# Attention scores in one two-bank PSUM tile, v's product on four quadrants, and one written order for the first layer

## The chip, the cores and the metric

One Trainium2 chip, one core of it. The metric is the device time of one execution in microseconds (us). The engines are TensorE (PE for matmuls, PEld for its weight loads), VectorE (DVE), ScalarE (ACT), GpSimd (POOL) and SyncE (SP, which here only issues DMAs).

## What is computed

Three stages follow one another, all in fp32: chunked attention, a gated layer (`x @ w_a * x @ w_b @ w_out`), and a mixture of four experts. The first two are called the first layer here, the third the second layer. The reference, cut:

```python
# attention: 4 batches, 8 heads, 576 positions in chunks of 64, head size 64
scores = scale * np.matmul(q_c, k_c.transpose(0, 1, 2, 4, 3))
scores = scores - np.max(scores, axis=-1, keepdims=True)
attn = np.exp(scores)
attn = attn / (np.sum(attn, axis=-1, keepdims=True) + 1e-09)
x = np.matmul(attn, v_c)                       # -> 2304 tokens x 512
x = ((x @ w_a) * (x @ w_b)) @ w_out            # 512 -> 1536 -> 512
p = domain_probs / (domain_probs.sum(-1, keepdims=True) + 1e-09)
for e in range(4):                             # 512 -> 1024 -> 512
    out += p[:, e:e + 1] * (np.maximum(x @ w1[e], 0.0) @ w2[e])
```

## The kernel before

**Numbers.** Each fp32 operand of the large products is kept as two fp32r tiles, a high part (a ScalarE copy) and a low part (the rest, a VectorE or GpSimd subtraction). Each product is then three matmuls: high by high, high by low, low by high. Some products of larger blocks go by a Strassen scheme with seven products for eight (`seq`, L845; `a_steps`, L1030; `o_step`, L1145). The weights of the first layer come in as float64 words and are turned into fp32 on the chip (`from_f64`, L227: two ScalarE, three VectorE and one GpSimd instruction for each piece of 512 columns), then split (`split_w`, L257). The weights of the second layer are split, summed and stored to DRAM by small jobs (`prepare`, L355) beside the first layer, and are loaded back later.

**Attention.** The 2304 tokens are 18 tiles of 128. For one tile, `emit_S` (L534) writes the scores into two PSUM tiles of one bank each, one for each head of a pair: 16 matmuls of 64x64x64, each of which the trace shows as two instructions. `emit_A` (L548) takes, for each of the two PSUM tiles, a maximum along the row and a subtraction, so four VectorE instructions on 256 columns. `emit_exp` is ScalarE's. `emit_B` (L565) sums the rows, adds, takes the reciprocal on VectorE and multiplies on GpSimd. `emit_T` (L575) transposes on TensorE and copies back on ScalarE. `emit_V` (L614) multiplies by v into one PSUM bank; its output goes to the same half of the partitions as its input comes from, so of the four 64x64 quadrants of the array only the two on the diagonal are in use. Two splits of the result (high part on ScalarE at once, low part on VectorE later) give x.

**PSUM.** The eight banks are four tiles `pm` (scores, the gated layer's a and b) and four tiles `ps` (transposes, v's product, w_out's products, the warm-up).

**Order.** The order of the instructions is the order in which the Python calls are made; every engine runs its own in order. The start is written out by hand (from L1279), with 40 warm-up matmuls that compute nothing (`keep_warm`, L204) between the attention of tiles 0 to 4. After that, eleven spans of the first two of twelve blocks of the gated layer run; between the steps of a span whole attention tiles are put in (`attn_slot`, L645), and w_out's steps of the span before are spread among them. Then the other ten blocks run in pairs (F = 1 to 5, L1377). Preparing jobs for the second layer come at written due counts (`WHEN`, L387; `tick`, L422, counts the steps). The jobs of the second layer itself (`part_of_h`, L1007: high and low parts of its hidden values, and sums) come when a small planner (`Plan`, L46) that follows instructions with estimated durations finds their engine free and their inputs ready.

Of the kernel before, what the change touches and what calls it, by code (L numbers as in the profile page):

```python
# [8 lines left out]
F32 = mybir.dt.float32  # L9
# [8 lines left out]
P = 128  # L18
# [3 lines left out]


DMA_US = 6.0
# [4 lines left out]
class Queue:  # L29
    def __init__(self, plan, name, engine):  # L30
        self.plan, self.name, self.engine = plan, name, engine

    def __getattr__(self, op):
        call = getattr(self.engine, op)

        def go(*args, **kw):
            aps = [x for x in (*args, *kw.values()) if isinstance(x, bass.AP)]
            out = kw.get("out", aps[0])
            ins = [x for x in aps if x is not out]
            self.plan.note(self.name, op, out, ins)  # L40
            return call(*args, **kw)  # L41

        return go


class Plan:  # L46


    LEAD = dict(PE=0.05, DVE=0.03, ACT=0.03, POOL=0.08, SP=0.05)

    def __init__(self, nc):
        self.nc = nc
        self.at = dict(PE=0.0, DVE=0.0, ACT=0.0, POOL=0.0, SP=0.0, port=0.0)
        self.written, self.read, self.writer, self.rings = {}, {}, {}, {}
        self.vector = Queue(self, "DVE", nc.vector)
        self.scalar = Queue(self, "ACT", nc.scalar)
        self.gpsimd = Queue(self, "POOL", nc.gpsimd)
        self.tensor = Queue(self, "PE", nc.tensor)
        self.sync = Queue(self, "SP", nc.sync)

    def __getattr__(self, name):
        return getattr(self.nc, name)

    def ring(self, tag, tile, n):

        names = self.rings.setdefault(tag, [])
        if len(names) >= n:
            old = names[-n]
            self.read[tile.tensor.name] = max(self.read.get(old, 0), self.written.get(old, 0))
        names.append(tile.tensor.name)  # L70
        return tile

    def cost(self, name, op, out, ins):

        n = out.free_size()
        psum = [x.space == bass.MemoryType.PSUM for x in (out, *ins)]
        if name == "PE":
            return ins[-1].free_size() / 2400 + 0.0134, False
        if name == "ACT":
            return (0.157 + n * 0.00084 if any(psum) else 0.172 + n * 0.00088), False  # L80
        if name == "POOL":
            return 0.18 + n * 0.00218, True
        n = max([n, *(x.free_size() for x in ins)])
        if any(psum):
            return 0.158 + n * 0.00104, False
        two = sum(x.free_size() > 1 for x in ins) > 1
        return (0.158 + n * 0.00104 if two else 0.15 + n * 0.00052), True

    def start(self, name, op, out, ins):
        t = self.at[name]  # L90
        deps = [self.written.get(x.tensor.name, 0) for x in ins]
        if self.writer.get(out.tensor.name) != name:
            deps.append(self.written.get(out.tensor.name, 0))
        deps.append(self.read.get(out.tensor.name, 0))
        t = max(t, max(deps) + self.LEAD[name])
        if self.cost(name, op, out, ins)[1]:
            t = max(t, self.at["port"])
        return t

    def note(self, name, op, out, ins):  # L100
        t = self.start(name, op, out, ins)
        if op == "dma_start":
            self.at[name] = t + 0.36
            end = t + DMA_US
        else:
            us, port = self.cost(name, op, out, ins)
            end = t + us
            self.at[name] = end if name == "PE" else end - 0.06
            if port:
                self.at["port"] = end - 0.14  # L110
            if name == "PE":
                end += 0.17
        self.written[out.tensor.name] = max(end, self.written.get(out.tensor.name, 0))
        self.writer[out.tensor.name] = name
        for x in ins:
            self.read[x.tensor.name] = max(end, self.read.get(x.tensor.name, 0))
# [3 lines left out]
def fused_kernel(  # L120
# [11 lines left out]

    nc = plan = Plan(tc.nc)
# [22 lines left out]
    ps_p = first.enter_context(tc.tile_pool(name="ps", bufs=4, space=bass.MemoryType.PSUM))  # L169
    early = ctx.enter_context(ExitStack())  # L170
    at_p = early.enter_context(tc.tile_pool(name="at", bufs=2, side="right"))
    st_p = early.enter_context(tc.tile_pool(name="st", bufs=3, side="right"))
# [3 lines left out]
    def psum():  # L176
        return plan.ring("ps", ps_p.tile([P, 512], F32, tag="ps", name="ps"), 4)

    def psum_m():
        return plan.ring("pm", psm_p.tile([P, 512], F32, tag="pm", name="pm"), 4)  # L180
# [23 lines left out]
    def keep_warm(n):  # L204

        ps = psum()
# [20 lines left out]
    def from_f64(r):  # L227
# [4 lines left out]
        nc.scalar.activation(out=low.bitcast(I32), in_=low, func=ACTF.Copy, scale=2.0**-29)  # L232
        nc.vector.tensor_single_scalar(out=high, in_=high, scalar=0x80000000, op=ALU.bitwise_and)
# [10 lines left out]
        )  # L244
        nc.gpsimd.tensor_tensor(
            out=t.bitcast(I32), in0=t.bitcast(I32), in1=low.bitcast(I32), op=ALU.add
        )
        load_w()
        return t
# [23 lines left out]
    def raw2_tile(name):  # L273
        return plan.ring("raw2", raw_p.tile([P, 1024], F32, tag="raw2", name=name, bufs=1), 1)
# [10 lines left out]
    def hi2(n, k):  # L285
        if nxt["prep"] == len(pieces):
            t = plan.ring("raw", raw_p.tile([P, 2, 512], F32R, tag="raw", name="made"), 2)
        else:
            t = plan.ring("made", made_tile(), 3)
        made[n, k] = t  # L290
        split_hi(t[:, 0, :], half(n, k))
# [11 lines left out]
    def sums2(n, x):  # L303
# [9 lines left out]
        if SUMS == "DVE":  # L313
            add_sb(o, y, z, op)
        else:
            nc.gpsimd.tensor_tensor(out=o, in0=y, in1=z, op=op)

    SUMS = "POOL"
    jobs = []
    EARLY = dict(ACT=0.05, POOL=1.8, DVE=0.05)  # L320
    SLACK = dict(ACT=0.9, POOL=3, DVE=0.9)

    class Job:
        def __init__(self, q, go, after=(), ready=lambda: 0, when=lambda: True, rank=0):
            self.q, self.go, self.after = q, go, after
            self.ready, self.when, self.rank, self.done = ready, when, rank, False
            jobs.append(self)

        def run(self):
            if not self.done:  # L330
# [3 lines left out]
                jobs.remove(self)  # L334
                self.go()

        def fits(self, now):
            if not (self.when() and all(j.done for j in self.after)):
                return False
            free = max(plan.at[self.q], plan.at["port"] if self.q != "ACT" else 0)  # L340
            if free > now + SLACK[self.q]:
                return False
            return self.ready() <= max(free, now) + EARLY[self.q]

    def written(tile):
        return plan.written.get(tile.tensor.name, 0)

    def over(tile):
        return max(written(tile), plan.read.get(tile.tensor.name, 0))

    def old(tag, back):
        return max([0] + [plan.read.get(x, 0) for x in plan.rings.get(tag, [])[-back:][:1]])


    def prepare(n, first):  # L355

        def fresh():
            return old("raw", 2) if nxt["prep"] == len(pieces) else old("made", 3)

        def job(q, go, after, ready):  # L360
            return Job(q, go, after, ready, rank=1)

        raw = lambda: written(raw2[n])
        before = job("ACT", lambda: load_raw2(n), first, lambda: old("raw2", 1))
        his, los = {}, {}
        stores = []
        for k in range(4):
            if k == 2:
                for x in range(4):
                    before = job(  # L370
                        SUMS,
                        lambda x=x: sums2(n, x),
                        (los[0], los[1]) if x == 0 else (before,),
                        lambda: over(raw2[n]),
                    )
            after = (before, *stores[-1:])
            his[k] = job("ACT", lambda k=k: hi2(n, k), after, lambda: max(raw(), fresh()))
            los[k] = job("POOL", lambda k=k: lo2(n, k), (his[k],), lambda k=k: over(made[n, k]))
# [1241 lines left out]
```

## Time and profile before

| what | us |
|---|---|
| median of three runs | 1226.9 (1226.55 to 1228.14) |
| the profiled execution | 1226.14 |
| its span, first to last instruction | 1224.4 |
| PE busy in the span | 1201.6 |
| DVE busy in the span | 841.3 |
| POOL busy in the span | 808.4 |

Matmuls are pipelined and overlap in the records, so a busy share of PE is not the share of its peak; the distance from one matmul's start to the next one's start tells how long one really takes. Idle time of an engine counts only where the end of the work waits for it.

### The profile page before, as it was taken

Reading aid. Unit: us, or ns where it says so; the run is one execution under the profiler, and the core shown is the slowest. Engines: PE = TensorE matmul, PEld = TensorE weight load, DVE = VectorE, ACT = ScalarE, POOL = GpSimd, SP = SyncE. Lnnn points to the kernel's source line nnn. Section 1 sums busy time; section 2 is a strip of 40 time slices with the busy share of each in tenths; the row PEclk is TensorE's granted clock in tenths of the full one; section 3 lists DMA queues with packets and bytes.
Section 4 is the critical chain, followed back from the end, with each engine's and each line's share of the span. In section 5 each row is a group of like instructions: output and inputs, shape, how many; then the busy total and the mean of one; then the engine's idle time right before and its main releaser. Section 6 shows DMA issues by size and latency. Waiting matters only on the chain.

```text
span 1224.4 us, 18164 instructions
## 1 busy us (share of the span) xinstructions
PE 1201.6 (98%) x6680; PEld 997.0 (81%) x6682; DVE 841.3 (69%) x1174; ACT 474.4 (39%) x858; POOL 808.4 (66%) x672
## 2 busy tenths in 40 slices
PE   7999999999999999999999999999999999999998
PEld 4877888888888888878888888888888888888886
DVE  7866458777647676636667666766788867768677
ACT  4645534444434443364333333333325233232331
POOL 4435566657466677588987897888657565565654
PEclk9999999999999999999999999999999999999999
DMA  7643432445345353778887887885448767666572
GB/s 254 227 169 130 175 120 87 147 162 169 106 163 179 140 190 137 259 285 315 292 302 285 332 298 243 299 303 189 155 159 306 289 209 241 211 236 230 200 251 93
DMA packets 76884, 261.35 MB, mean 213 GB/s; under 512 B 8610, under 2 KB 8682, under 8 KB 76796
## 3 DMA queue, kind: packets, MB, share of 16 engines
q1 hardware_dynamic: 53756, 176.30, 42.1%
q10 hardware_dynamic: 23040, 83.90, 18.4%
q8 instruction: 53, 0.87, 0.3%
q14 instruction: 35, 0.29, 0.1%
HBM read 188.29 MB, written 71.86 MB: 212 GB/s over the span
## 4 chain that ended last, share of the span: by engine, by line
PE 81%; DVE 7%; POOL 4%; issue 3%; ACT 2%; DMA 2%; POOLq 0%; ACTq 0%; SPq 0%; DVEq 0%
PE pm L41 43%; PE po L41 27%; PE ps L41 11%; POOL made L41 2%; POOL raw L41 1%; DVE t L41 1%; DVE d L41 1%; DMA raw<-in_w2p_dram 1%; DVE sm L41 1%; DVE mx L41 1%; DVE raw L41 1%; DVE pm L41 1%; DMA w<-kept 1%; DVE cB L41 0%; POOL w L41 0%
## 5 line engine op out<-in xcount | busy, mean ns | idle before, releaser
L41 DVE TENSOR_TENSOR y<-po,y 128x1024 f32<-128x1024 f32 (+1 forms) x207 | 249.8, 1208 | 127.6 <-PE po L41 127.5
L41 POOL TENSOR_TENSOR made<-raw,made 128x512 fp32r<-128x512 f32 x128 | 168.8, 1332 | 70.7 <-ACT made L41 69.8
L41 PE MATMUL pm<-cB,w 128*128 128x512 f32 (+1 forms) x768 | 190.8, 384 | 0.3 <-DVE g L41 0.3
L41 PEld LDWEIGHTS pm<-cB,w 128*128 128x128 f32 x768 | 140.0, 188 | 27.7 <-DVE g L41 0.5
L41 PE MATMUL pm<-cT,w 128*128 128x512 f32 x582 | 149.4, 392 | 0.0
L41 PE MATMUL ps<-gh,w 128*128 128x512 f32 (+1 forms) x488 | 138.1, 366 | 0.1
L41 PE MATMUL pm<-xh,w 128*128 128x512 f32 (+1 forms) x576 | 134.6, 355 | 0.0
L41 PEld LDWEIGHTS pm<-cT,w 128*128 128x128 f32 x582 | 108.5, 188 | 24.4 <-ACT m L41 0.9
L41 PE MATMUL po<-hT,w 128*128 128x512 f32 x486 | 123.5, 389 | 0.0
L41 PEld LDWEIGHTS pm<-xh,w 128*128 128x128 f32 x576 | 98.6, 189 | 16.3
L41 ACT CAST made<-raw 128x512 fp32r<-128x512 f32 x128 | 76.4, 621 | 91.4 <-DMA raw<-in_w2p_dram 37.3
L41 POOL TENSOR_TENSOR raw<-raw 128x256 f32<-128x256 f32 x128 | 100.7, 787 | 9.4
L41 PEld LDWEIGHTS po<-hT,w 128*128 128x128 f32 x486 | 91.2, 188 | 19.1
L41 POOL TENSOR_TENSOR t<-t,raw 128x512 int32<-128x512 int32 x36 | 48.4, 1344 | 81.5 <-issue 26.6
L41 POOL TENSOR_TENSOR hB<-m,hB 128x512 fp32r<-128x512 f32 x63 | 81.7, 1298 | 29.4 <-ACT hB L41 29.4
L41 PEld LDWEIGHTS ps<-gh,w 128*128 128x128 f32 x488 | 87.9, 188 | 15.4 <-POOL w L41 0.5
L41 PE MATMUL po<-hB,w 128*128 128x512 f32 x384 | 99.1, 393 | 0.0
L41 DVE TENSOR_TENSOR xacc<-ps,xacc 128x512 f32<-128x512 f32 (+1 forms) x112 | 67.6, 626 | 44.9 <-PE ps L41 44.9
L41 PE MATMUL ps<-ag,w 128*128 128x512 f32 (+1 forms) x244 | 90.5, 371 | 4.7 <-DVE ag L41 2.4
L41 POOL TENSOR_TENSOR hT<-m,hT 128x512 fp32r<-128x512 f32 x62 | 80.9, 1310 | 19.0 <-ACT hT L41 13.3
L41 PEld LDWEIGHTS po<-hB,w 128*128 128x128 f32 x384 | 72.1, 188 | 16.2
L41 POOL TENSOR_TENSOR m<-m,u 128x512 f32<-128x512 f32 x31 | 41.3, 1331 | 64.6 <-DVE g L41 64.3
(153 smaller groups left out, 2262.2 us busy)
## 6 DMA issues: line engine op xcount, KB each, us to landing
w<-kept SPq DMA_DIRECT2D x179, 512.0 KB, 4.9
kept<-made ACTq DMA_DIRECT2D x128, 512.0 KB, 2.9
made<-kept SPq DMA_DIRECT2D x77, 512.0 KB, 4.7
raw<-in_w1p_dram SPq DMA_DIRECT2D x36, 512.0 KB, 3.6
raw<-in_w2p_dram ACTq DMA_DIRECT2D x32, 512.0 KB, 5.4
q<-in_q_dram SPq DMA_DIRECT2D x18, 256.0 KB, 4.7
k<-in_k_dram SPq DMA_DIRECT2D x18, 256.0 KB, 4.6
v<-in_v_dram SPq DMA_DIRECT2D x18, 256.0 KB, 4.3
```

Of the source, the lines that this page charges most:

```text
L41: return call(*args, **kw)
```

## The change

- `emit_S` writes the scores of a tile into one PSUM tile of two banks. The bank is (i + c) mod 2, for head i of the pair and chunk c, where before it was i. `emit_A` becomes one maximum and (`emit_D`) one subtraction on 512 columns.
- `emit_V` writes chunk c into bank c of such a two-bank tile, and the output's half of the partitions is i xor c: all four quadrants are used. The host swaps v's halves for the second chunk accordingly.
- PSUM while attention runs: two of these two-bank tiles (`pd`, a ring for both scores and v's product) and the four tiles `pm`, which now hold the transposes and w_out's products as well. From the token `mid` on, the four `ps` tiles are back.
- The parts of the steps get names of one letter: S scores, A maximum, D subtraction, E exp, B row sum, R reciprocal, M normalisation, T transpose, C copy, V v's product, H and L high and low part of x; c, d, g, h, l the parts of a weight's conversion and split; w, q, v loads; a, b, x the products, t, g, i, j, y their ends. One string, `START`, of 1,961 such names gives the order of the whole first layer. It holds no warm-up matmul.
- `WHEN` has new due counts, and they now cover the second layer's jobs too; the planner is gone. x's low part is a plain VectorE subtraction where it was a fused one.

The diff, cut to its core:

```diff
     def emit_S(t):
-        att[t] = ps = [psum_m()[:, : HP * CH].rearrange("p (a n) -> p a n", a=HP) for _ in range(2)]
+        ps = psum_2()
+        att[t] = ps[:, :, : HP * CH].rearrange("p b (a n) -> p b a n", a=HP)
...
-                        out=ps[i][n, hp, :], lhsT=qq[s, hp, n], rhs=kk[s, hp, n], start=True, stop=True
+                        out=att[t][n, (i + c) % 2, hp, :],
+                        lhsT=qq[s, hp, n],
+                        rhs=kk[s, hp, n],
...
     def emit_A(t):
-        for i, ps in enumerate(att[t]):
-            m = mx[:, :, i : i + 1]
-            nc.vector.tensor_reduce(out=m, in_=ps, axis=AX.X, op=ALU.max)
-            nc.vector.tensor_tensor(
-                out=dd[:, :, i, :], in0=ps, in1=m.to_broadcast([P, HP, CH]), op=ALU.subtract
-            )
+        nc.vector.tensor_reduce(out=mx, in_=att[t], axis=AX.X, op=ALU.max)
+    def emit_D(t):
+        nc.vector.tensor_tensor(
+            out=d.rearrange("p (a h) n -> p h a n", h=2),
+            in0=att.pop(t),
+            in1=att_d[t].to_broadcast([P, 2, HP, CH]),
+            op=ALU.subtract,
+        )
...
     def emit_V(t):
-        ps = psum().rearrange("p (a n) -> p a n", a=HP)
+        ps = psum_2()[:, :, : HP * CH].rearrange("p c (a n) -> p c a n", a=HP)
...
-                    s = slice(CH * i, CH * i + CH)
+                    s, o = (slice(CH * y, CH * y + CH) for y in (i, i ^ c))
                     nc.tensor.matmul(
-                        out=ps[s, hp, CH * c : CH * c + CH],
+                        out=ps[o, c, hp, :],
                         lhsT=vv[s, c, hp, :],
-                        rhs=aT[s, hp, CH * c : CH * c + CH],
+                        rhs=aT[s, hp, n],
...
-        make_identity(tc.nc, ident)
-        load_qk(0)
-        keep_warm(12)
...
+    START = """
+        q0 S0 A0 D0 q1 S1 A1 q2 E0 B0 R0 M0 S2 A2 w w c D1 D2 d g E2 B2 T0 C0 E1 B1 R1 h M1 q3 S3 A3
+        c v0 V0 H0 q4 v1 D3 E3 d T1 R2 q5 S4 L0 . . . . C1 V1 H1 M2 T2 B3 R3 L1 a0.0 A4 D4 g w S5 A5
+        q6 l c d M3 g a0.1 a0.2 E4 v2 h . T3 C3 B4 D5 . C2 R4 v3 S6 A6 l w E5 B5 a0.3 v4 V2 b0.0
...
     def tick():
         count[0] += 1
-        now = plan.at["PE"]
-        while jobs_1 and WHEN[jobs_1[0][0]] <= count[0]:
-            jobs_1.pop(0)[1].run()
-        while True:
-            j = next((j for j in jobs if not j.rank and j.fits(now)), None)
-            if j is None:
-                return
-            j.run()
+        for n in due.get(count[0], ()):
+            jobs[n].run()
```

## Rows read from the trace of the kernel before

**Rows 1.** The page: busy time of each engine, and the granted clock in 40 slices.

```profile
PE 1201.6 (98%) x6680; PEld 997.0 (81%) x6682; DVE 841.3 (69%) x1174; ACT 474.4 (39%) x858; POOL 808.4 (66%) x672
...
PEclk9999999999999999999999999999999999999999
```

**Rows 2.** Windows, eight stages of the span; columns in the first row.

```profile
core 0: us, PE busy (x) PEld busy (x) DVE busy (x) ACT busy (x) POOL busy (x), PEclk, DMA share, GB/s
0.00:21.85 21.85, 17.44 (x275) 10.31 (x277) 15.04 (x33) 8.79 (x14) 6.62 (x12) 1.00 0.81 276
21.85:40.00 18.15, 14.14 (x250) 11.96 (x248) 16.12 (x39) 9.63 (x20) 10.00 (x9) 1.00 0.70 222
40.00:120.00 80.00, 75.57 (x1032) 63.13 (x1032) 55.99 (x137) 41.55 (x92) 35.55 (x34) 1.00 0.50 173
120.00:350.00 230.00, 229.86 (x1080) 191.86 (x1081) 150.62 (x226) 97.96 (x180) 140.32 (x118) 1.00 0.41 139
350.00:523.00 173.00, 170.61 (x848) 143.00 (x847) 113.16 (x173) 72.46 (x133) 117.51 (x99) 1.00 0.51 180
523.00:550.00 27.00, 25.48 (x122) 21.13 (x123) 9.16 (x15) 16.77 (x26) 22.56 (x20) 1.00 0.75 277
550.00:1200.00 650.00, 649.69 (x3003) 540.59 (x3002) 462.05 (x533) 225.04 (x393) 466.80 (x379) 1.00 0.72 253
1200.00:1224.40 24.40, 18.78 (x82) 15.02 (x81) 19.21 (x23) 2.22 (x4) 9.01 (x5) 0.95 0.25 86
```

**Rows 3.** Groups by form, PE in 21.85 to 120 us; five of thirteen rows.

```profile
L41 PE MATMUL pm<-cB,w 128*128 128x512 f32 x72 | 19.3, 396 | 0.0
L41 PE MATMUL ps<-aT,v 64*64 64x64 f32 x512 | 18.4, 221 | 2.2 <-ACT xacc L41 2.2
L41 PE MATMUL ps<-ident,d 128*128 128x128 f32 x63 | 10.2, 284 | 0.6 <-POOL d L41 0.6
L41 PE MATMUL pm<-k,q 64*64 64x64 f32 x416 | 10.1, 224 | 1.8 <-issue 0.9 <-DVE d L41 0.8
...
L41 PE MATMUL pm<-xl,w 128*128 128x256 f32 x16 | 3.1, 295 | 0.9 <-DVE xl L41 0.9
```

**Rows 4.** Timeline of PE: start, length, instruction; six rows of 82 to 90 us.

```profile
82.21 0.84 PE L41 MATMUL pm<-cB,w 128*128 128x512 f32 x3
...
82.89 0.39 PE L41 MATMUL ps<-ag,w 128*128 128x512 f32 x1
...
87.06 0.69 PE L41 MATMUL pm<-k,q 64*64 64x64 f32 x32
87.68 0.66 PE L41 MATMUL ps<-ident,d 128*128 128x128 f32 x4
88.27 1.15 PE L41 MATMUL ps<-aT,v 64*64 64x64 f32 x32
89.35 1.65 PE L41 MATMUL pm<-cB,w 128*128 128x512 f32 x6
```

**Rows 5.** Timeline of PE, the start: warm-up matmuls and the first product of the layer.

```profile
0.77 4.04 PE L41 MATMUL ps<-const-bfloat16-1.0 128*128 128x512 bf16 x12 [0.77 <-PEq L1601]
...
7.98 2.13 PE L41 MATMUL ps<-const-bfloat16-1.0 128*128 128x512 bf16 x9 [0.16 <-issue]
...
21.85 1.20 PE L41 MATMUL pm<-xh,w 128*128 128x256 f32 x8
```

**Rows 6.** Timeline of DVE: maximum, subtraction and row sum of one tile.

```profile
12.70 0.42 DVE L41 TENSOR_REDUCE mx<-pm 128x4 f32<-128x256 f32 x1
13.15 0.42 DVE L41 TENSOR_TENSOR d<-pm,mx 128x256 f32<-128x256 f32 x1
...
14.28 0.67 DVE L41 TENSOR_REDUCE sm<-d 128x8 f32<-128x512 f32 x1
```

**Rows 7.** Waits of PE over the span: in total, times, longest (us).

```profile
PE po L41 <- POOL hB L41: 1.5, 1, 1.5
...
PE pm L41 <- DVE d L41: 0.8, 2, 0.5
```

More of the change, by code (lines that the diff above doesn't have):

```diff
@@ L46 @@
[L46 to L116, printed above, removed]
@@ L348, in over @@
[L348 to L352, printed above, removed]
-    def prepare(n, first):
[L357 to L366, printed above, removed]
+    def prepare(n, first):
+        before = Job(lambda: load_raw2(n), *first)
+        los, stores = {}, []
@@ L454, in load_l2 @@
                 while (g, k) not in saved:
-                    next(j for j in jobs if j.rank).run()
+                    next(j for j in jobs if not j.done).run()
                 t = made_tile() if len(l2_loads) % 10 in (2, 5, 8) else w_tile()
@@ L764, in step @@
                 sub_hi(nc.gpsimd, l, ac, h)
-        return [lambda dd=dd: step(dd) for dd in range(KD)]
+        return step, add_up
     def combos(b11, b21, b12, b22, t_at, eng_b=nc.gpsimd, eng_t=nc.vector):
@@ L1153, in o_step @@
         h = H.pop((o, part))
-        used.add((o, part))
         bh, bl = h[:, 0, :], h[:, 1, :]
-        ps = plan.ring("po", late["ps"].tile([P, 2, 512], F32, tag="po", name="po"), 2)
+        ps = late["ps"].tile([P, 2, 512], F32, tag="po", name="po")
         for d in range(2):
@@ new lines, in fused_kernel, with name, conv, to_mid @@
+    """
+    with tc.manual_schedule():
+        make_identity(nc, ident)
+        do = {}
+        def name(n, go):
+            do[n] = go
+        name("k", lambda: keep_warm(1))
+        name("w", load_w)
+        turn, done, split = [], [], []
+        def conv(x):
+            if x == "c":
+                key = pieces[nxt["begin"]]
+                nxt["begin"] += 1
+                turn.append((key, f64_a(raws[key].pop(0))))
+                done.append(turn[-1])
+                ready[key] = turn[-1][1][0]
+                if key[1] > 1:
+                    f32s[key[1] // 2, 2 * key[2] + key[1] % 2] = ready[key]
+            elif x == "d":
+                f64_d(*turn.pop(0)[1])
+            elif x == "g":
+                f64_g(*done.pop(0)[1])
+            elif x == "h":
+                key = pieces[nxt["prep"]]
+                nxt["prep"] += 1
+                t = w_tile()
+                split_hi(t[:, 0, :], ready[key])
+                split.append((ready.pop(key), t))
+                wts[key] = (t[:, 0, :], t[:, 1, :])
+            else:
+                src, t = split.pop(0)
+                sub_hi(nc.gpsimd, t[:, 1, :], src, t[:, 0, :])
+        for x in "cdghl":
+            name(x, lambda x=x: conv(x))
+        for t in range(NT):
+            name(f"q{t}", lambda t=t: load_qk(t))
+            name(f"v{t}", lambda t=t: load_v(t))
+            for x, go in zip("SADEBRMTCVHL", (emit_S, emit_A, emit_D, emit_exp, emit_B, emit_R, emit_M, emit_T, emit_C, emit_V, emit_H, emit_L)):
+                name(f"{x}{t}", lambda go=go, t=t: go(t))
+        name("probs", lambda: nc.sync.dma_start(out=pr, in_=probs.rearrange("p (t e) -> p t e", e=E)))
+        name(".", tick)
+        name("prep", prepare_all)
+        name("sums", domain_probs)
+        name("rows", probs_rows)
+        def to_mid():
+            early.close()
+            late["sums"] = first.enter_context(
+                tc.tile_pool(name="ps", bufs=4, space=bass.MemoryType.PSUM)
+            )
+            late["mid"] = mid.enter_context(tc.tile_pool(name="mid", bufs=1, side="right"))
+        name("mid", to_mid)
@@ L1464, in fused_kernel @@
+        name("late", to_late)
+        name("W", load_l2)
+        for n in START.split():
+            do[n]()
+        x2, add_up = x2_steps((2 * NP1 - 2, 2 * NP1 - 1), 0, 0, blocks[0][1])
+        x2 = [lambda dd=dd, x2=x2, y=add_up: (x2(dd), y(dd)) for dd in range(KD)]
         load_l2(4)
```

604 lines of the change are left out of this document (259 added, 345 removed), and 94 rows, old and new, of the table WHEN.

## The prediction

> **What bounds the kernel now.** I read the page first, then windows by stage, then the groups by form and the timelines inside the stages that lose time. The page [rows 1] shows PE busy in 98% of the span, so only two things can shorten it: less work for PE, or less time in which PE has none. The windows [rows 2] show where the latter lies. PE's idle time (length less busy) is 4.4 us up to 21.85, 4.0 us from there to 40, 4.4 us from 40 to 120, 0.1 us in the 230 us after that, 2.4 us from 350 to 523, 1.5 us in 523 to 550, where the second layer begins, 0.3 us in the next 650 us, and 5.6 us at the end, which is the last sums and their store. So the second layer is full and the first 120 us are not. In those, DVE is busy 16.1 of 18.15 us up to 40 and 56.0 of 80 us after: it paces the attention early and has room later.
>
> Busy is not the same as well used. Before 21.85 most of PE's busy time is warm-up: the first product of the layer starts only there [rows 5]. After that a start-to-start count tells more. Three 512-column matmuls take 0.68 us, 0.227 each, and one tile costs 0.62 for scores, 0.59 for transposes, 1.08 for v's product [rows 4]. Between 21.85 and 120 the groups by form hold 133 products of 512 columns and 144 of 256 in ten groups, of which the first and the last are shown, 512 instructions of v's product (16 tiles of 32), 416 of scores (13 tiles) and 63 of transposes (16 tiles of four, one not recorded) [rows 3]. With 256 columns taken at half of 0.227, that is 133 x 0.227 + 144 x 0.114 + 16 x 1.08 + 13 x 0.62 + 16 x 0.59 = 81.4 us of 98.15. So 16.7 us of this stage are lost, about half of them as visible idle.
>
> **The change part by part.**
>
> *v's product on four quadrants.* Scores and v's product have the same count and shape, 32 instructions of 64x64x64 a tile. Scores alternate over four quadrants and take 0.62 us, v's product uses two and takes 1.08 [rows 4]. I take the scores' rate for the new one: 0.46 us a tile. The nearest row is the same stream on all quadrants; the other end is no gain at all (0), since nothing in the trace separates the quadrants from the banks. Two of the 18 tiles lie before 21.85, where PE has slack. 16 x 0.46 = 7.4 us, on the path where PE is the limit. Up to 40, where DVE paces, some of it turns into waiting, and this is in the next item's bounds.
>
> *Two VectorE instructions fewer a tile.* Two maxima and two subtractions on 256 columns take 14.28 - 12.70 = 1.58 us from start to start. A reduction over 512 columns takes 0.67 [rows 6], so one maximum and one subtraction on 512 columns should take some 1.3. That frees 0.28 x 18 = 5 us of DVE, most of it in the stage where DVE is busy 89%. It costs one new thing: scores and subtraction are no longer overlapped by halves, which is some 0.4 us of latency a tile (one 256-column instruction [rows 6]), and hidden as long as another tile's work is there.
>
> *The order.* Finer pieces and one order for loads, conversions, attention and products can use the 16.7 lost us of 21.85 to 120. I take 8 us of it (the visible idle of that stretch is 8.4 us, and what DVE is freed of is 5 us). Bounds: 0, if each wait filled is replaced by another; 12, since the products still need x. From 120 to 523 the visible idle is 2.5 us; I take 1.5 back, bounds -2.5 and +4 (a new order can also make gaps where there are none). The wait at the start of the second layer is 1.5 us, almost all in one wait of PE on GpSimd's low part [rows 2, 7]; I take 0.5 back, bounds -1.5 and +1.
>
> *The start without warm-up.* The new order puts before the first product the same attention work as before: scores of five tiles, transposes of three, v's product of two. DVE has the same list there with four tiles' maxima and subtractions merged, 1.1 us less, and is busy 15.0 of the 21.85 us. So the first product can come some 1 us earlier. Removing the 40 matmuls frees PE in a stretch where PE is not the limit, which is worth nothing by itself. What they may have done is the clock: of the recorded warm-up matmuls the first 12 take 4.04 us, 0.34 each, nine later ones 2.13 us, 0.24 each [rows 5]; 512 columns at 2.4 GHz are 0.213 us and at 1.2 GHz 0.427, so the first ones ran partly at the lower level, while the granted clock in the profile stands at full in every stage but the last [rows 1, 2]. Without them scores, transposes and v's product may run at the lower level until the products begin and some way into them. I price this at +2 us, bounds 0 and +5 (below). Start in all: +1, bounds -2 and +5.
>
> The Trainium skill ("TensorE: Matmul & The Clock Gate", Part 1) says that the throttled clock is the default and that activity releases it. The slow first 12 matmuls agree; no row of this trace shows an attention start without them.
>
> *w_out's products and transposes in `pm`.* Four banks now serve a, b, w_out's steps and transposes, and two two-bank tiles serve scores and v's product. PE takes its instructions in order, so a score matmul that waits for VectorE's subtraction two uses back holds every product queued behind it. Before, PE waited for that subtraction twice, 0.8 us in all [rows 7], because the scores shared four banks with a and b. I take 0 for it beside the 8 us above; the price if it fails is the slower rival.
>
> *Fixed due counts in the second layer.* The planner's choices become constants. The stage has 0.3 us of idle in 650 [rows 2], so there is nothing to win and I take 0; bounds 0 and +16 (0.5 us in each of 32 rounds).
>
> Sum: -7.4 - 8 - 1.5 - 0.5 + 1 = -16.4. The profiled execution took 1226.14 us, 1.7 more than its span of 1224.4, and the median of the runs is 1226.9, 0.8 above it. 1226.1 - 16.4 = 1209.7, so 1210.
>
> **The rivals.**
> 1. *The forecast*, 1210. Bounds: 1226.1 - 2 - 7.4 - 12 - 2.5 - 1.5 = 1201 at best.
> 2. *The order gives nothing back*: only the quadrants count, 1226.1 - 7.4 + 1 = 1220. For it: half of the visible idle of that stage lies before 40, where DVE is busy 89% and no order makes it faster. Against: the other half lies beyond 40, where DVE is busy 70% [rows 2].
> 3. *The clock stays low*: from the first product to 40 us PE would do its work at half rate. In the whole stage the work is 81.4 of 89.7 us busy, so of the 14.1 us busy before 40 [rows 2] some 12.8 are work; at half rate that is 25.6, 7.5 more than the stretch has. As the clock rises once PE is full, as it did within the first 12 warm-up matmuls [rows 5], I take 5: 1210 + 5 = 1215.
> 4. *The banks, not the quadrants, set the rate of the small matmuls*: scores write head i to bank i now, v's product everything to one bank. After, two halves of the rows of the array write to one bank in both. Then v's product keeps 1.08 and scores rise to it: 1210 + 7.4 + 13 x 0.46 = 1223. The Trainium skill ("TensorEngine Tiling (Array Packing)", Gotcha 1: PSUM Pressure) has such a rule: different row tiles write to different banks and can't use one bank at the same time. The old scores obey it and are the fast ones, the old v's product doesn't and is the slow one; so the rows fit it as well as they fit the quadrants.
> 5. *The ring of two* (slower): scores and v's product take the two-bank tiles in turn, 36 times. Each use waits for VectorE to have read the tile two uses earlier, and VectorE's queue holds weight conversions and the gates of the layer in front of it. It decides from 16.4 / 36 = 0.46 us a use; at 0.9 us, one 512-column instruction of 0.67 us [rows 6] and some 0.25 of passing it on, it costs 32 us: 1242. For it: 89% busy DVE up to 40. Against: only 0.8 us of such waits now [rows 7], with the same number of banks.
> 6. *The fixed due counts come late in the second layer*: 32 rounds of 0.5 us, 1210 + 16 = 1226. GpSimd is busy 72% there [rows 2], so it has room, and this is unlikely.
>
> **How the numbers follow.** Forecast 0.54, order without gain 0.15, clock 0.08, banks 0.06, ring 0.10, due counts 0.07. A measurement can tell about 0.2% from no change, which is 2.5 us: 1224.4 to 1229.4 is the same. Faster are the first four but for a part of the banks' case (0.02), with a tenth part of the due counts: 0.81. The same: that 0.02, half of the due counts and the edge of the second case, 0.07. Slower: the ring and the rest, 0.12. The range goes from 1201, the forecast's best, to 1223, the banks' case; it leaves out the ring, most of the due counts and some beyond the best, less than 0.2.
>
> **What would show each step.** In the profile after: v's product at about 0.62 us a tile from start to start, and scores still there; one maximum and one subtraction a tile at about 0.68 each; the first product at 20 to 23 us; PE's idle from there to 120 below 5 us; 120 to 523 with 1 us; the second layer with 0.3. The clock would show as scores of 1 us or more a tile before the first product, and products of 256 columns at 0.2 us after it. The forecast is wrong if PE waits for the subtraction or for x's low part at scores and v's product, or if the second layer shows waits on GpSimd or ScalarE that it has not now.

## The result and the profile after

The changed kernel takes 1208.5 us (1206.8 to 1210.3 in four runs) where the kernel before takes 1227.5: a ratio of 0.9845, 95% interval 0.9825 to 0.9865, which is 19.0 us (16.6 to 21.5). Two more sets of runs of it, with the experiments below, gave 1209.3 (0.9855, 0.9834 to 0.9876) and 1207.5 (0.9839, 0.9825 to 0.9852). The profiled execution took 1209.71 us, its span is 1207.9.

The page of the changed kernel: busy time of the engines, to stand beside [rows 1].

```profile
PE 1185.3 (98%) x6642; PEld 988.9 (82%) x6642; DVE 832.8 (69%) x1138; ACT 473.3 (39%) x858; POOL 808.8 (67%) x672
```

PE is busy 16.3 us less, and the span is 16.5 us shorter. So PE's idle time in all is the same, 22.8 us before and 22.6 after, but it lies elsewhere, as the windows show. They are cut at the first product of the layer, the last of v's products, the start of the second layer and the ends of the stretch with gaps in it; columns as in [rows 2]:

```profile
0.00:20.18 20.18, 10.44 (x237) 8.79 (x237) 13.09 (x27) 8.72 (x15) 6.48 (x12) 1.00 0.86 298
20.18:40.00 19.82, 18.26 (x374) 16.04 (x373) 19.00 (x45) 15.33 (x34) 12.79 (x12) 1.00 0.90 295
40.00:100.50 60.50, 59.35 (x897) 49.34 (x896) 44.08 (x96) 35.32 (x75) 31.60 (x31) 1.00 0.54 175
100.50:503.00 402.50, 402.22 (x1951) 338.20 (x1942) 268.84 (x405) 173.60 (x319) 263.38 (x220) 1.00 0.46 161
503.00:530.00 27.00, 27.00 (x131) 22.68 (x130) 8.86 (x15) 17.05 (x27) 23.43 (x23) 1.00 0.88 328
...
600.00:920.00 320.00, 315.73 (x1502) 263.47 (x1501) 216.89 (x256) 113.28 (x199) 238.81 (x195) 0.99 0.71 253
```

Between the first product and the last of v's products PE now idles 19.82 - 18.26 = 1.6 us and 1.2 us, where it was 4.0 and 4.4 [rows 2]. From there to the second layer it idles 0.3 us, where it was 2.5. The 1.5 us of idle at the start of the second layer are gone (503 to 530). In their place stand 9.7 us of idle before the first product, where the kernel before has 4.4 beside its warm-up matmuls, and 4.3 us in the second layer between 600 and 920, which was full before.

The same in landmarks of PE's timeline, each the start of an instruction but for the last two:

| landmark | before | after | lead | e5: order alone | e8: parts alone |
|---|---|---|---|---|---|
| first product of the layer | 21.85 | 20.18 | 1.7 | 21.1 | 21.2 |
| first matmul into `po` (second layer) | 524.6 | 503.2 | 21.4 | 510.1 | 522.2 |
| end of PE's last matmul | 1218.8 | 1202.3 | 16.5 | 1207.4 | 1218.0 |
| end of the span | 1224.4 | 1207.9 | 16.5 | 1213.0 | 1223.5 |

The number of products before `po` is 2,220 in each of the four. So the first layer is 21.4 us ahead, and the second gives 4.9 back: from `po` to PE's end it takes 694.2 us before and 699.1 after. The column e5 is the new order with the new division of PSUM, the new due counts and no warm-up, but without the cheaper parts.

The small matmuls in PE's timeline of the changed kernel (start, length, instruction), beside [rows 4]:

```profile
16.91 1.13 PE L422 MATMUL pd<-k,q 64*64 64x64 f32 x32
18.35 1.13 PE L519 MATMUL pd<-aT,v 64*64 64x64 f32 x32 [0.30 <-issue]
19.41 1.11 PE L474 MATMUL pm<-ident,d 128*128 128x128 f32 x4
20.18 1.01 PE L602 MATMUL pm<-xh,w 128*128 128x256 f32 x3
...
23.38 0.69 PE L422 MATMUL pd<-k,q 64*64 64x64 f32 x32
24.00 0.62 PE L602 MATMUL pm<-xl,w 128*128 128x256 f32 x3
...
28.95 0.69 PE L519 MATMUL pd<-aT,v 64*64 64x64 f32 x32
29.57 0.66 PE L474 MATMUL pm<-ident,d 128*128 128x128 f32 x4
```

From start to start v's product is 29.57 - 28.95 = 0.62 us, scores 24.00 - 23.38 = 0.62. Before the first product both are slower: v's product takes 19.41 - 18.35 = 1.06. That is the lower clock of a start without warm-up. In this profile the granted-clock column reads 1.00 up to there and doesn't show it, as it didn't for the first warm-up matmuls [rows 5]; in a second profile of the same kernel (c0 below) it does, with the same 1.06 us for v's product (18.22 to 19.28):

```profile
17.40:24.20 6.80, 5.98 (x81) 5.44 (x81) 6.56 (x13) 2.96 (x6) 4.54 (x4) 0.50 0.94 296
```

VectorE's groups up to 100 us in the changed kernel (count, busy, mean ns, idle before), beside [rows 6]:

```profile
L439 DVE TENSOR_TENSOR d<-pd,mx 128x512 f32<-128x512 f32 x18 | 12.1, 683 | 0.8
L434 DVE TENSOR_REDUCE mx<-pd 128x8 f32<-128x512 f32 x18 | 12.1, 672 | 7.9 <-PE pd L422 7.9
```

And PE's waits over the span (total, times, longest), beside [rows 7]:

```profile
PE pd L422 <- DMA k<-in_k_dram: 5.7, 2, 4.5
PE pm L474 <- POOL d L466: 3.5, 2, 1.8
PE po L1012 <- POOL hB L106: 2.4, 2, 2.2
PE po L1012 <- POOL hT L106: 1.9, 2, 1.2
PE pd L519 <- DVE sm L459: 1.1, 1, 1.1
PE pd L519 <- DVE d L439: 0.3, 1, 0.3
```

The first two lie in the start, before the first product, where the kernel before ran warm-up matmuls. For a two-bank tile (`pd`) PE waits on VectorE twice at v's product, 1.4 us in all; on GpSimd's low parts in the second layer 4.3 us in four waits, where the kernel before has one of 1.5 [rows 7].

### The profile page after: what moved, and what is told of

Same layout as the page of the kernel before. It is cut to its first block, busy times and chain, and to the rows that moved or that the text cites. A ratio compares the mean times of both kernels' runs of the same rounds, so it can differ in the third digit from the quotient of the medians.

```text
span 1207.9 us, 17954 instructions
## 1 busy us (share of the span) xinstructions
PE 1185.3 (98%) x6642; PEld 988.9 (82%) x6642; DVE 832.8 (69%) x1138; ACT 473.3 (39%) x858; POOL 808.8 (67%) x672
## 4 chain that ended last, share of the span: by engine, by line
PE 84%; POOL 5%; DMA 5%; DVE 3%; issue 2%; ACT 1%; POOLq 0%; SPq 0%; ACTq 0%; DVEq 0%
PE pm L719 26%; PE po L1012 20%; PE pm L602 17%; PE ps L556 4%; PE ps L557 3%; PE ps L558 3%; PE po L1084 3%; DMA raw<-in_w2p_dram 2%; PE ps L719 2%; DMA kept<-made 2%; POOL made L106 2%; PE pm L556 2%; PE pm L558 1%; PE pm L557 1%; POOL hT L106 1%
## 5 line engine op out<-in xcount | busy, mean ns | idle before, releaser
L719 PE MATMUL pm<-cB,w 128*128 128x512 f32 x552 | 140.7, 390 | 0.0
L719 PEld LDWEIGHTS pm<-cB,w 128*128 128x128 f32 x552 | 102.7, 188 | 20.8
L602 PEld LDWEIGHTS pm<-xh,w 128*128 128x128 f32 x576 | 99.0, 189 | 16.4
L1012 PEld LDWEIGHTS po<-hT,w 128*128 128x128 f32 x480 | 90.0, 188 | 19.8 <-POOL hT L106 1.0
L1012 PE MATMUL po<-hB,w 128*128 128x512 f32 x366 | 94.7, 394 | 0.2 <-POOL hB L106 0.2
L1012 PEld LDWEIGHTS po<-hB,w 128*128 128x128 f32 x366 | 68.6, 188 | 16.0 <-POOL hB L106 0.7
L95 DVE TENSOR_TENSOR xacc<-ps,xacc 128x512 f32<-128x512 f32 (+1 forms) x100 | 60.7, 629 | 28.3 <-PE ps L558 28.3
L556 PE MATMUL ps<-ag,w 128*128 128x512 f32 (+1 forms) x208 | 77.2, 371 | 0.3 <-DVE xacc L95 0.3
L557 PE MATMUL ps<-gh,w 128*128 128x512 f32 (+1 forms) x208 | 76.9, 370 | 0.0
L558 PE MATMUL ps<-gh,w 128*128 128x512 f32 (+1 forms) x208 | 76.7, 369 | 0.0
L602 PE MATMUL pm<-xl,w 128*128 128x512 f32 (+1 forms) x288 | 72.8, 356 | 0.0
```

Source lines behind the costliest of these rows:

```text
L95: nc.vector.tensor_tensor(out=out, in0=in0, in1=in1, op=op)
L556: nc.tensor.matmul(out=ps[:, :n], lhsT=wh, rhs=al, start=(m == 0), stop=False)
L557: nc.tensor.matmul(out=ps[:, :n], lhsT=wh, rhs=ah, start=False, stop=False)
L558: nc.tensor.matmul(out=ps[:, :n], lhsT=wl, rhs=ah, start=False, stop=(m == last))
L602: nc.tensor.matmul(out=st[i][:, :n], lhsT=x, rhs=y, start=m == 0, stop=m == 3 * KD - 1)
L719: nc.tensor.matmul(out=ps, lhsT=x, rhs=y, start=first and kk == 0 and m == 0, stop=kk == 1 and m == 2, skip_group_check=not first,)
```

## The experiments

Each was timed against the kernel before on the same chip, and three sets of runs give the changed kernel itself. All ratios are to the kernel before.

**c0 and c1, the changed kernel again.** No edit.

> The changed kernel as it is, beside the experiments of this call, so that each stands against it on the same chip: 1208 us, some 19 below the kernel before.

> The changed kernel as it is, beside the two experiments of this call: 1206 to 1214, median 1209; from the first matmul of the second layer to PE's last one 694 to 699 us.

Measured 1209.3 (single runs 1206.3 to 1214.4) and 1207.5 (1205.9 to 1208.2). From `po` to PE's end the profiles have 696.9 and 696.3 us. So the second layer of the changed kernel is not the same in every execution: 699.1, 696.9, 696.3, against 694.2 before.

**e1, v's product back on two quadrants.** In the changed kernel:

```diff
-                        out=att[t][n, (i + c) % 2, hp, :],
+                        out=att[t][n, i, hp, :],
...
-                    s, o = (slice(CH * y, CH * y + CH) for y in (i, i ^ c))
+                    s, o = (slice(CH * y, CH * y + CH) for y in (i, i))
...
-    vv[:, 1] = vv[:, 1, ::-1].copy()
```

> The changed kernel with v's product on the two diagonal quadrants again, still into two banks in the same sequence of banks, and scores with head i in bank i. Theory (quadrants set the rate): v's product goes from 0.62 back to 1.08 us a tile and the time up by some 6 to 7 us, to 1215. Rival (banks set it): v's product stays at 0.62 and the time at 1208.

Measured 1213.2 us, ratio 0.9896 (0.9878 to 0.9915). One tile of v's product and two in a row, in PE's timeline of e1:

```profile
29.24 1.15 PE L519 MATMUL pd<-aT,v 64*64 64x64 f32 x32
30.32 0.66 PE L474 MATMUL pm<-ident,d 128*128 128x128 f32 x4
...
50.69 2.08 PE L519 MATMUL pd<-aT,v 64*64 64x64 f32 x64
52.70 0.38 PE L556 MATMUL pm<-ag,w 128*128 128x256 f32 x1
```

One tile takes 30.32 - 29.24 = 1.08 us again, and two in a row 52.70 - 50.69 = 2.01, a little over 1.0 each; scores keep their 0.62 (47.98 to 48.60 in the same timeline). The banks are the same, in the same sequence (0, 0, 1, 1); only the half of the partitions that the second chunk goes to has changed. So the quadrants set the rate. The banks' rival falls. The Trainium skill ("TensorEngine Tiling (Array Packing)", Gotcha 1: PSUM Pressure) has it that different row tiles can't use one bank at the same time. That didn't cost anything here: in the changed kernel both halves of the rows write to one bank right after one another (banks 0, 0, 1, 1), and v's product runs at the 0.62 us of scores, whose two halves write to different banks (0, 1, 1, 0). The second layer of e1 begins at 510.0, 6.8 us later than in the changed kernel's profile and 5.0 later than in the profile of c0 (505.0), near the 7.4 that the prediction gave for it. The median is 3.9 us above that of c0 on the same chip; the profiles show part of why it is less: from `po` to PE's end e1 takes 695.0 us and c0 696.9.

**e2, four VectorE instructions a tile again.** In the changed kernel:

```diff
-        nc.vector.tensor_reduce(out=mx, in_=att[t], axis=AX.X, op=ALU.max)
+        for b in range(2):
+            nc.vector.tensor_reduce(
+                out=mx[:, b], in_=att[t][:, b], axis=AX.X, op=ALU.max
+            )
...
+        for b in range(2):
+            nc.vector.tensor_tensor(
+                out=dd[:, b],
+                in0=ps[:, b],
...
```

> The changed kernel with two maxima and two subtractions on 256 columns a tile, as before the change. Theory of the record (half of the order's gain is what VectorE is freed of): some 0.28 us a tile come back on VectorE, 5 us, of which up to 4 reach the end: 1213. Rival: the new order has VectorE off PE's path after 30 us, and only the first tiles count: 1209 to 1210, first product some 0.5 us later.

Measured 1208.0, ratio 0.9841 (0.9828 to 0.9855): no difference from the changed kernel that intervals of some 1.7 us either way can tell. The first product starts at 20.23 (20.18 before the edit), the second layer at 503.8 (503.2). The rival holds, and even its half microsecond at the first product is not there: in the new order the VectorE time that the merging frees is on nobody's path.

**e5, the order alone.** Both edits, e1 and e2, together.

> The changed kernel with both of the above undone: two diagonal quadrants for v's product, scores with head i in bank i, four VectorE instructions a tile; PSUM's use and the order are the new ones. Theory: the order alone brings what the record gave it and the two parts add up: 1227 - 10 = 1217. Rival: the parts overlap (with slower parts the order has nothing to fill): 1222.

Measured 1214.8, ratio 0.9899 (0.9885 to 0.9913): 12.4 us below the kernel before, by the ratio, without any of the cheaper parts. Its windows, from its first product on:

```profile
21.10:40.00 18.90, 17.29 (x361) 15.60 (x359) 18.12 (x50) 13.74 (x32) 10.48 (x10) 0.99 0.84 272
40.00:107.60 67.60, 66.48 (x909) 56.51 (x909) 46.83 (x118) 37.17 (x78) 33.93 (x32) 1.00 0.52 173
107.60:510.00 402.40, 402.12 (x1947) 338.29 (x1944) 268.89 (x405) 173.54 (x318) 262.95 (x220) 1.00 0.46 160
```

PE's idle is 1.6, 1.1 and 0.3 us, as small as with the cheaper parts, while VectorE is busy 18.1 of 18.9 us up to 40. The order, with the PSUM division and the due counts that come with it, removes the gaps by itself.

**e8, the parts alone.** The kernel before, with the two-bank scores, the merged VectorE instructions and the four quadrants, the PSUM tiles divided as in the change while attention runs, and the old order:

```diff
...
+    pd_p = early.enter_context(tc.tile_pool(name="pd", bufs=2, space=bass.MemoryType.PSUM))
...
+                        out=ps[n, (i + c) % 2, hp, :], lhsT=qq[s, hp, n], rhs=kk[s, hp, n], start=True, stop=True
...
+                        out=ps[CH * (i ^ c) : CH * (i ^ c) + CH, c, hp, :],
...
```

> The kernel before with the two-bank scores, the two VectorE instructions fewer and v's product on four quadrants, in its own old order (PSUM as after the change while attention runs; warm-up, planner and due counts as before). Theory of the record: 7 us from the quadrants and little from VectorE without a new order: 1227 - 7 = 1220. Rival: in the old order the ring of two two-bank tiles and w_out's products in the four other banks make PE wait, and the gain is lost: 1225 or more.

Measured 1224.3, ratio 0.9979 (0.9970 to 0.9988): 2.6 us. Outside the stretches at half clock v's product is as fast as in the changed kernel (37.04 to 37.67, 0.63 us), so 7 us of PE's work are gone, and the time with them is not. Its windows from the first product on, one wait of PE with VectorE's work before it, and two lines of PE's waits from 21 to 121 us:

```profile
21.20:40.00 18.80, 15.58 (x249) 13.26 (x247) 16.34 (x33) 10.21 (x21) 11.24 (x10) 0.73 0.74 244
40.00:117.20 77.20, 70.50 (x1031) 58.27 (x1030) 52.73 (x114) 40.36 (x90) 33.93 (x33) 0.98 0.52 174
...
90.77 0.66 PE L41 MATMUL pm<-ident,d 128*128 128x128 f32 x4
94.71 1.13 PE L41 MATMUL pd<-aT,v 64*64 64x64 f32 x32 [3.28 <-issue]
...
93.97 0.64 DVE L41 TENSOR_TENSOR xl<-pd,xh 128x512 fp32r<-128x512 f32 x1
...
PE pd L41 <- issue: 6.1, 4, 3.3
...
26.50:36.70 10.20, 9.17 (x145) 7.84 (x136) 8.68 (x20) 5.75 (x14) 5.90 (x5) 0.50 0.65 222
94.80:98.20 3.40, 3.40 (x38) 2.80 (x39) 1.84 (x4) 1.62 (x3) 2.85 (x4) 0.51 0.77 209
```

PE idles 3.2 and 6.7 us in the first two windows, where the kernel before has 4.0 and 4.4 [rows 2]. The longest wait ends when VectorE has finished x's low part, out of the two-bank tile, at 93.97 + 0.64 = 94.61, and PE starts at 94.71; VectorE had a weight's conversion, a sum and a row sum in front of that. The other three waits end in the same way, 0.1 us after VectorE's last read of a two-bank tile: a subtraction for scores (29.93, PE at 30.03) and a low part for v's product twice (51.42, 51.51; 60.92, 61.02). This is the prediction's ring of two, in the old order. The last two lines show a second loss: the granted clock is at half (1.2 GHz) for 10.2 us after the sparse stretch before it, and for 3.4 us right after the wait of 3.3 us, although this kernel has its warm-up. How much of the missing gain is the ring and how much the clock was not separated. In these windows, from 21.2 to 117.2, PE idles 9.9 us, only 1.5 more than the 8.4 of the kernel before, so in this execution the ring's waits stand largely in the place of others; the two stretches at half clock hold 9.17 + 3.40 us of PE's work, of which half, 6.3 us, is an estimate of the most that the clock can have cost. Against the clock: over the eleven runs the mean granted clock goes from 0.993 to 0.997, and the times do not follow it (1224.3 to 1225.3 at 0.993, 1224.1 at 0.997).

**e3, warm-up put into the changed kernel**, 38 matmuls at the places of the kernel before:

```diff
-        q0 S0 A0 D0 q1 S1 A1 q2 E0 B0 R0 M0 S2 A2 w w c D1 D2 d g E2 B2 T0 C0 E1 B1 R1 h M1 q3 S3 A3
-        c v0 V0 H0 q4 v1 D3 E3 d T1 R2 q5 S4 L0 . . . . C1 V1 H1 M2 T2 B3 R3 L1 a0.0 A4 D4 g w S5 A5
+        q0 k12 S0 A0 D0 q1 S1 k9 A1 q2 E0 B0 R0 M0 S2 k8 A2 w w c D1 D2 d g E2 B2 T0 C0 E1 B1 R1 h M1 q3 S3 A3
+        c v0 V0 k5 H0 q4 v1 D3 E3 d T1 k4 R2 q5 S4 L0 . . . . C1 V1 H1 M2 T2 B3 R3 L1 a0.0 A4 D4 g w S5 A5
...
```

> The changed kernel with 38 warm-up matmuls put in at the places where the kernel before has them (12 before the first scores, 9, 8, 5 and 4 later). Theory: the lower clock before the first product lengthens a chain that passes through TensorE ten times, about 0.45 us each time, of which half is hidden behind VectorE: the first product comes 1 to 2 us earlier than 20.2 and the time falls by as much, to 1206.5. Rival: the loads and VectorE set the first product; the warm-up changes nothing or stands in the way of the scores: 1208 to 1210.

Measured 1207.3, ratio 0.9839 (0.9825 to 0.9852), inside the spread of the changed kernel; it is 2.0 us below c0 on the same chip, with intervals that overlap. The first product starts at 20.29, no earlier than without (20.18), though scores and v's product before it run at 0.62 us. The second layer starts at 504.1, where the three profiles of the changed kernel have 503.2, 505.0 and 503.9. In PE's timeline and the windows of e3:

```profile
18.89 0.69 PE L519 MATMUL pd<-aT,v 64*64 64x64 f32 x32 [0.33 <-issue]
19.52 0.66 PE L474 MATMUL pm<-ident,d 128*128 128x128 f32 x4
20.29 0.61 PE L602 MATMUL pm<-xh,w 128*128 128x256 f32 x3
...
20.29:27.10 6.81, 4.69 (x113) 3.92 (x114) 6.60 (x15) 4.24 (x8) 4.71 (x5) 1.00 0.63 211
27.10:30.60 3.50, 3.50 (x52) 3.28 (x55) 3.21 (x9) 2.04 (x6) 2.41 (x3) 0.51 0.96 280
```

With warm-up the clock falls to half at 27.1, after a stretch in which PE was busy 4.69 of 6.81 us. So in this profile the warm-up moves the low clock from before the first product to behind it, and neither the first product nor the second layer starts earlier for it.

**e6, the kernel before without warm-up.** The `keep_warm` calls of the start taken out, nothing else.

> The kernel before without its 40 warm-up matmuls, nothing else changed. Theory after the run with warm-up put in (the first product did not come earlier): the lower clock costs nothing there, the loads and VectorE set the first product: 1226 to 1228. Rival (the record's +2 us): scores and v's product at the lower clock come later by some 0.5 us each on the chain: 1229.

Measured 1229.4, ratio 1.0014 (1.0005 to 1.0023): 1.7 us slower, 0.6 to 2.8. In its timeline and windows:

```profile
22.42 1.11 PE L41 MATMUL ps<-ident,d 128*128 128x128 f32 x4
23.19 2.05 PE L41 MATMUL pm<-xh,w 128*128 128x256 f32 x8
...
19.70:26.50 6.80, 6.27 (x98) 5.66 (x94) 6.56 (x12) 3.18 (x6) 4.93 (x5) 0.50 0.88 311
```

The first product starts 23.19 - 21.85 = 1.3 us later [rows 5], at half clock; the second layer starts 0.7 us later (525.3 against 524.6), and from there the profile takes 0.9 us more. So in the old order the price of a cold start, 1.7 us, is near the +2 that the prediction gave for the new one, with 0.7 of it seen in the first layer; in the new order none was measured.

**e4, the old moments in the second layer.** The changed kernel with the due counts at which the kernel before ran its jobs, from the second layer's first step on (645 numbers of `WHEN`).

> The changed kernel with the due counts of the kernel before from the second layer on (the moments that its planner chose there, and its preparing jobs in that stage); the first layer is untouched. Theory: the new fixed counts are what the second layer loses. Between the product that has 3000 after it and the one that has 1500 after it the changed kernel loses 6.7 us against the kernel before; with the old counts this comes back and PE's waits on GpSimd (4.3 us in four waits) go: 1208 - 6 = 1202, and 0.3 us of idle from 550 to 1180. Rival: the loss comes with the earlier start of the second layer (the stored weights and GpSimd's backlog are not as far), so that the old counts wait as much: 1208.

Measured 1212.7, ratio 0.9877 (0.9858 to 0.9896). The theory falls: from `po` to PE's end it takes 702.2 us, not less than with the new counts, and the median is 3.4 us above c0's on the same chip. PE's longest waits in e4 from 500 to 1182 us:

```profile
PE pm L719 <- DVE hl L1063: 2.7, 1, 2.7
PE po L1012 <- POOL hT L106: 1.6, 3, 0.7
PE po L1012 <- POOL hB L106: 1.5, 1, 1.5
```

The moments that were nearly free of waits in the kernel before are not free of them when the stage begins 20 us earlier.

**e9 and e10, other moments in the second layer.** In the changed kernel, e9 has the first edit, e10 both:

```diff
-        for n in due.get(count[0], ()):
+        for n in sorted(due.get(count[0], ()), key=lambda n: n < 17 * len(todo)):
...
     for n, t in enumerate(WHEN):
+        if n < 17 * len(todo) and t > 600:
+            t += 2
```

> The changed kernel; where jobs of the second layer and its preparing jobs are due at the same step, the second layer's go first. Theory: PE's waits on GpSimd in the second layer come from casts for the stored weights, which wait on ScalarE for their tile and hold the casts of the hidden values behind them; with the order turned the waits get shorter: some 1.5 us less, 1207. Rival: the waits come from GpSimd's order over several steps or from the transfers; same time and same waits, 1209.

> As the one before, and the preparing jobs due after step 600 come two steps later. Theory: a cast that is issued later waits less for the store in front of it, so less of ScalarE's queue is held: 1206. Rival: the stored weights then come late for their loads and PE waits for these: 1212.

Measured for e9 1209.7, ratio 0.9863 (0.9847 to 0.9879), against 0.9839 of the changed kernel (c1) on the same chip; from `po` to PE's end 696.5 us against 696.3. Its theory falls. For e10 1235.9, ratio 1.0076 (1.0064 to 1.0089): 28 us slower than the changed kernel for a shift of two steps. PE's longest waits from 500 us on, e9 and then e10, and for e10 a cast of ScalarE and a window before its longest wait:

```profile
PE po L1012 <- POOL hT L106: 2.2, 2, 1.8
...
PE po L1014 <- POOL hT L106: 15.3, 5, 10.5
PE pm L721 <- ACT u L926: 4.4, 2, 2.4
PE pm L721 <- ACT m L919: 3.0, 1, 3.0
...
768.03 0.62 ACT L92 CAST made<-raw 128x512 fp32r<-128x512 f32 x1 [8.50 <-DMA kept<-made]
...
760.00:768.00 8.00, 4.84 (x27) 3.89 (x26) 2.82 (x4) 0.00 (x0) 0.12 (x1) 1.00 0.99 359
```

The rival of e10 was late weights; PE waits for no load of weights there, but for GpSimd and ScalarE. Behind its longest wait, 10.5 us up to 775.3, stands a store: a cast for a stored weight waits 8.50 us for it on ScalarE, with the DMA engines at 0.99 from 760 to 768, GpSimd waits 8.66 us for that cast, and the low part that PE needs comes behind it in GpSimd's queue. So the theory has the wrong sign: from 500 to 900 us ScalarE's casts wait 47.4 us for stores in e10 and 31.3 in the changed kernel. The clock is at half for 10.2 us from 768.2 on, on top of the wait.

## Why the prediction was right

The sum said 16.4 us and the two profiled executions differ by 1226.14 - 1209.71 = 16.4. That this fits to the tenth is luck, twice over. By the ratios the change is worth 18 to 20 us, and of the changed kernel's three profiles the one compared has the slowest second layer. And the parts were off and cancel: up to the start of the second layer the sum had 7.4 + 8 + 1.5 - 1 = 15.9 us, and the profiles have 21.4, 19.6 (c0) and 20.7 (c1); the second layer, priced at 0, then gives 4.9, 2.7 and 2.1 back.

- **v's product** (7.4): right in mechanism and nearly in size. 1.08 to 0.62 us a tile, as the row of scores gave it; undoing it moves the second layer's start by 5 to 6.8 us and the median by 4 to 6. The bound of 0, and the banks as the cause, are excluded by e1. What the step left out is the condition: in the old order the same part brought 2.6 us together with the others (e8).
- **VectorE's merging** (part of the 8): wrong as a cause. The instructions merged as forecast (0.67 and 0.68 us), and nothing that was measured followed from it (e2); in e2 the four instructions keep VectorE busy 26.5 us over the 18 tiles, only 2.3 more than the two, where the step took 5 (in the kernel before, where a maximum and a subtraction alternate, it is 29.8). Reading a busy share of 89% up to 40 us as the limit was the step that failed: in the changed kernel VectorE is busy 19.0 of 19.8 us there, more than before, and PE idles less. In e5, with all four instructions, it is busy 18.1 of 18.9 us, and PE idles as little. A busy engine was not a late one. That it was the place of its instructions in the queue is what is left, and e5 fits it.
- **The order** (8, then 1.5 and 0.5): right in mechanism, and too small. Alone it gives 12.4 us (e5), and the visible idle between the first product and the second layer goes from 11.0 us [rows 2] to 3.0. The 2.5 us of gaps after 120 went nearly all, where 1.5 were taken, and the 1.5 at the start of the second layer all, where 0.5 was. The 16.7 lost us that the step drew on were miscounted: the ten groups hold 145 products of 512 columns, not 133 (one of the two groups of 12 was left out), so the work is 84.1 us and the loss 14.0. Counted in the same way from the first product to the last of v's products (136 products of 512 columns in the new order, 145 in the old, and v's product at 0.62 where it has four quadrants), e5 has 82.1 us of work in 86.7, a loss of 4.6, and the changed kernel 74.7 in 80.4, a loss of 5.7. So the order took 9.4 of 14.0 us. e8 has 76.8 us of work in 96.2 and loses 19.4: most of what the cheaper parts freed there was lost again. 12.4 and 2.6 make 15.0, less than the 18 to 20 of the whole change by its three ratios; the intervals hardly tell this from none, but the start of the second layer shows it as well (14.5 and 2.4 us ahead, against 19.6 to 21.4). So the cheaper parts look worth more in the new order. That in the old one PE waits for the two-bank tiles and the clock falls (e8) fits this, and which of the two counts was not separated.
- **The start** (+1): the other way round, -1.7. The first product comes at 20.18, though the small matmuls before it run at the lower clock. It comes at 20.23 without the merging (e2) and at 20.29 with warm-up (e3), inside the 20.0 to 20.2 of the three profiles of the changed kernel or next to it, so neither matters; 0.7 of the 1.7 us are the order's (e5: 21.1). Of the rest 0.3 goes with the quadrants alone (e1: 20.51), and what takes the other part is open. The clock's +2 is near what it costs in the old order (e6: 1.7), and was not found in the new (e3). The clock's rival (5 us) did not come: by 22 us (24 in c0) the clock is up, and five products of 256 columns from 22.04 to 22.73 take 0.14 us each, against 0.23 at half clock (e6).
- **The ring of two**: near the 0 of the forecast for the changed kernel (1.4 us in two waits), and real in e8 (6.1 us in four waits). The rival was right about the mechanism and wrong about where it would strike; its 0.25 us of passing a tile on is 0.1 in e8.
- **The second layer** (0, bounds to +16): inside the bounds, and the forecast's worst miss beside the order. Of the prediction's own signs of being wrong it is the one that plainly came: waits on GpSimd that it had not before. 699.1 - 694.2 = 4.9 us in the profiled execution: 4.3 us of waits on GpSimd where the kernel before idles 1.8 us from `po` on, and a stretch at half clock after the longest wait. Two other profiles lose 2.7 and 2.1, and e1, e2, e3 and e5, which have the same second layer, 0.8, 1.9, 0.8 and 3.1. The kernel before has this spread in part too: without warm-up (e6) it takes 695.1, with the cheaper parts (e8) 695.8. So the 4.9 of the first profile is the far end, and most of it is not a fixed price.

Windows of the changed kernel around that wait, columns as in [rows 2]:

```profile
800.00:810.00 10.00, 7.82 (x40) 6.35 (x39) 4.07 (x5) 3.50 (x7) 5.93 (x6) 1.00 1.01 384
810.00:814.00 4.00, 4.00 (x13) 3.10 (x12) 1.22 (x1) 1.19 (x3) 4.00 (x4) 0.57 0.64 260
```

PE has 7.82 of 10 us busy, the DMA engines are full (384 GB/s), and then the clock is near half. In these us ScalarE's casts for the stored weights wait 2.3 and 2.5 us for the store that holds their tile, GpSimd waits 2.0 and 2.1 us for those casts, and the low part that PE waits for (2.2 us, up to 809.5) stands behind them in GpSimd's queue; over 500 to 900 us ScalarE waits like this:

```profile
ACT made L92 <- DMA kept<-made: 31.3, 19, 6.7
```

In the kernel before it is 25.0 us in 17 waits over the same stage. **What stays open** is what makes these waits reach PE in some executions and by how much: neither the old moments (e4) nor the order within a step (e9) changed it for the better, and delaying the preparing jobs (e10) made it much worse, through GpSimd and ScalarE. That full transfers start it is argued from these lines and those of e10's longest wait; a kernel with more tiles for the stored weights would tell it apart and wasn't tried.

## What to carry to other kernels

A cheaper instruction is worth its time only where the next instruction is ready: the same parts gave 2.6 us in the old order, and in the new one the change went from the 12.4 us of the order alone to 18 to 20, so measure a part in the order it will live in. Ask of a busy engine not how full it is but whose instruction stands behind whose in its queue; taking 36 instructions off VectorE, which is busy 96% from the first product to 40 us, moved nothing in the new order. When one stage moves, hand-set moments in the next are a risk to be costed: a shift by two steps cost 28 us here.

## What the runs showed of the hardware

- Four quadrants against two: 16 matmuls of 64x64x64 (32 instructions in the trace) take 0.62 us, against 1.0 to 1.08 on the diagonal quadrants, with the same banks in the same sequence (e1).
- At the lower clock the same 16 take 1.06 us, and a 128x256 matmul 0.23 us (e6: eight from 23.19 to 25.04).
- Warm-up did not hold the clock. With it the clock fell to half later, at 27.1 (e3) and at 26.5 for 10.2 us (e8), after stretches in which PE was busy 69% (e3, 20.29 to 27.10) and 58% (e8, 3.1 of the 5.3 us from 21.2 to 26.5); without it the clock was at half from 19.7 to 26.5 (e6). The Trainium skill ("TensorE: Matmul & The Clock Gate", Part 1) has activity as what releases the clock. The starts agree: with warm-up v's product before the first product takes 0.63 us (e3), without it 1.06. The clock can fall inside an otherwise full stage too: PE idled 2.2 us up to 809.5 in the changed kernel, and the granted clock is 0.57 from 810 to 814.
